# All 64 weighted sums as six full-fp32 products in two halves of the array's columns, and a plan without shifts

## The chip, the cores and the metric

The kernel runs on one core of a Trainium2 chip. The metric is the device time of one execution in microseconds, taken as the median over several runs. The core has a matrix engine (TensorE, PE in the profile; its weight loads are PEld), a vector engine (VectorE, DVE), a scalar engine (ScalarE, ACT), GpSimd (POOL) and a sync engine (SyncE, SP) that issues all DMAs here. They run side by side, each works through its own queue in order, and they wait for one another by semaphores. Matrix products are written to PSUM, eight banks of 512 fp32 columns on 128 partitions.

## The reference

```python
# attention: q, k, v are (8, 8, 576, 64), s is (8, 8, 576)
scores = scale * q @ k.T                      # causal, 576 x 576
cum    = cumsum(max(s, 0))
scores = where(causal, -1e9, scores + min(-(cum_i - cum_j), 0))
attn   = exp(scores - rowmax) / (rowsum + 1e-9)
x      = attn @ v                             # the weighted sum, 64 heads
# gated MLP on x as (8, 576, 512)
h      = gelu(x @ w_in)                       # 512 -> 1024
u, v   = halves of h;  v_n = layernorm(v) * g_ln
v_s    = w_sg @ v_n + b_sg                    # over the sequence
out    = x + (u * v_s) @ w_out
```

## The kernel before, in words

One head at a time is attended to, in batches of eight heads; the MLP ("ffn") of a batch runs while the heads of the next batches are worked on. For a head, `scores` forms q·k in pieces (PSUM tiles `pss`), adds the mask and takes the row extreme on VectorE, takes the exponential and its sum on ScalarE, and `norm` scales the rows by the reciprocal sums. `context` then makes the weighted sum. The probabilities (tiles `p`, and `e` for a third set that the first heads use) are transposed by TensorE in 13 blocks of 128x128 or smaller through two PSUM banks (`psp`), copied to SBUF (`pa`, `pb`, `pd`), and multiplied with the head's values (`vs`) into one PSUM bank (`psx`). The result is put into `xr`, half a tile per head. Queries are split in five row tiles and keys in five column tiles of 128 (the last of 64), and only the causal part is computed: the products have 512, 448, 320, 192, 64 and 64 columns.

The kernel has two ways to make that sum. The first 12 heads (`NP = 12`) use full fp32: the values are the stationary operand, 64 columns wide, and each product goes to one half of the array's columns (`side` 0 is PSUM partitions 0 to 63, `side` 1 is 64 to 127). The products come in two groups, the second of which ends with a product on 64 rows (`k=REM`). An fp32 product shows as two MATMUL records. The other 52 heads split every operand into a high and a low part in the reduced type fp32r: the values' high and low parts stand side by side in the 128 columns of the array (`split_v`, ScalarE and GpSimd), and the transposed probabilities' high and low parts (`pah`, `pal`, `pbh`, `pbl`, `pdh`, `pdl`) are streamed one after the other. That is ten products per head, spread over five steps, with the splitting on ScalarE and VectorE, and two more evacuations at the end. The MLP uses fp32r pairs as well (tiles `psm`), three products for each.

The order of the work is not the order of the code. All calls are collected in a `Plan` as operations with dependencies; the positions `POS` give the order in which they are collected. `Plan.order` simulates the five engines with the costs of `cost` and list-schedules them in a few rounds; `nc.group()` binds calls to one operation that nothing is put into. Before the last round each operation's priority is moved by an entry of the table `SHIFT` times 200 ns. The table unpacks to 7,972 entries between -45 and 45, and the 1,929 that are not zero all lie in the first 2,046. The order is then issued as it stands, so every engine's queue is fixed.

`norm` scales row tile 3 (448 columns) on ScalarE for the first 12 heads (`'n0': 'gggsg'`) and on GpSimd for the others (`'n': 'ggggg'`).

Of the kernel before, what the change touches and what calls it, by code (L numbers as in the profile page):

```python
# [64 lines left out]
SHIFT = (  # L65
    'c-rmM=gxu*wgq4mM4Amm6h#pWDzEo{Au5Vkuwg;Lf*?gWUruI{lbmF3V0`}Uto3_kfA)dhS0~s$EDC)_QP{?iA~VUw*M$%49_cZ|XV<;?@|v)&'
    '>R%GB9gu@xJ%e(`kP>!d$W7O$3N_DF^Y0W)G@Euz`D<%3JCd9Uw8pLbDi_q=?e>lfiO9bkl9IT}8_)0$`hp)JX3Z^6ZbqvO(v;?%{_G`;xu6GB'
    'oqSE+VoZHGE*!(IUo`jlmpKheeqIul+Cy%$x_gR+^5R8TP_x_pupXYwMi8>y)a9$8Z##=VP*7kL&ZHTqp?{_k%&JBFaY6FgmENDIe*}$v^5lR;'
    '%Su62Z01q8Q}4rTx4TdU9+QHdZz_?K2;?+qT>f(QXd!mr^=cLvf$h!tktHR&KAd$`o-{Hyc651S=ylG&%Z)|0nAZv9s1!MGb?iSHi1OAG7rSW2'
    '^UWl2m4)kWl6s_^XQTBAkt&VM2$-y4z1wZ-eAb=C^M*RZO602Du^Ym-XTI+*Hp(YoS12wA?a9yN)jnErup$;Nj*2w*Y!pMG{w{;lcbZM!jgM<&'  # L70
    'MPY`Q^60V(9oh^g916EeO@-8q(9d41g1xP4WE~u=<umpOwD2;YlxxFhGIOewYxkt9?N>PcW_Olc{0xsBnIsba5XM(1os?*@d&R%zakez8Sa#H?'
    '9llUN*F;&i`dSAX40E8N^a|0wy*YsHl&zkla><4@CV;^Q|MZ}&$W_vMuST04o@G;-Dt^TaQhMfVLX2$2eZ&^p#z-6@K<;)Xm~u0nd#Ptnsh8P%'
    '*JehSwnnwnz3EHP?#zcGvjL@DL^QclSwp9t%7i>VDdi4rl4Ys%xjlt|0H4QpM_neRlX*P}Wf1tg@YiAX$m)k)al8va5Y^n`G({g$eCy6G&hzK7'
    'd`$`ZCf!VtX1`}9`};pmqSniI%7xj&-JbTw->Eeftyaq^L1lATcE=Ywo1Sv9+AMc29J$*f8kT(4!_nSCx|I%98h#u#<+_dC8oibVG`sDD<CQ=z'
    'J)o9ZnLrZdN4CyO?boAKZA4!`k|vKzfKMB2?P>)c=ymX0^-K^>tCq`UU}xU=Lb_Lpy~8Apm6xoggPX#N=IMA&5dH>N4|s4gwqMP*pu||P*L1bn'
    'p!kBI%)ME0*8@x_s&8kQ1^CjgQo1FwxV^t1Q8*^4OmG|(xlv{Psj$UsbI%AdNIa0)mKbbDH0#&aD$^M|3lA?EC%N#q`Ka9|H_G59iun<2&|&Yr'
    'J+n;?uh6emE1mHx{r!9U@ZI-Pgm2?{9zF4QJ=W*OBGEh?x*|0&*`pXQTKU7PpKD-&bPGowcV{+Vgg>d4)SsWw)2LzTNQv)p5v_y$W$vsbAxTd('
    '{qcY+^OI=}K<v&wlvV$A4=Z^`f&uk_rg}YqrV34Y9FY){<Xfp~du3`#d9@<zJg4B=Jp7z*dSLmF!k=Z#ggQ3v*G>rU5X3-9m8CGPy}d8J5L23?'
    'i~Y?%-zuV7<N`KyCr$7|lR^x&XtZ-XG6-f9r<^WN+IZX{p?of5q>9weYwvbC^Jg=996_@3JTAQX<$x>;?O8l=Hv*cBMi{<Bg_4#!#N~NH!%$o='
    '43Dx$b4&D}y}z~)PU#5+>QJNmr?S(^XS7<McG%gNv-Q&TYaEcSS7l;CY|_5AG27t#<OIWQ_M{}ZQhT&4&S&92%QR=wZcx-{G*j6RS>`0hYg~F?'  # L80
    ')9CTKlU0_|y;1*VJ0)NlqKGzt4Iz?~H`>SIp4S%PD*v}~@LOU1$@PLAlU-p)5m?UDw*!t5E0=D9v@p2zw#dB*U+PupOwP>;s}~Y--|(N1d4H_j'
    '$jf_!nn3})wLJ%$WDLu`*Q_}2tMCxN**XZ8;xO?gaG^u0-@j7?+?N%=DJ8Oi2c(nE<As}NE0IVq96jxdL3FYMeX9e-9A#z^lzYB%c}R|Ycp1Am'
    '3|>4;iWlL^XYLW7V4<6|8X+*vQaQJlT{ak@Gv?MbDY&8adaF*9!ibi0zTeyruus6*JOGeg1XwzAEqcG)P&+-V_s_&$SSb3jD4+Iy05Gy<6DTmi'
    'y~1{>gxdxbH<1bn&Dypet{u$Pt+KiR5r#{?5AM^zw>dw4t8VD0z>K#4Zi1u<Tv7l5fItuU|FD$uzt<=L7GV6leRc-`Xa6gh{2llY(6~(epC|%9'
    'KR-V|KR-V|KR-V|KR-V|KR-V|KmWD<2cC(<Py'
)
# [245 lines left out]
def cost(o, eng, kind, outs, ins, kw):  # L332
    n = _cols(outs[0])
    if eng == "PE":
        w = _cols(kw["in_"] if kind == "transpose" else ins[0])
        if kind == "transpose":
            o.pes.append((85.0 * w / P, 58.0, 165.0))
        elif ins[0].dtype == F32R:
            o.pes.append((max(54.0, 0.836 * w), 0.4397 * n + 6.4, 165.0))
        else:  # L340
            x = 0.47 * n + 45 if w == D else 0.83 * n + 95
            o.pes.append((107.0, x, 0.0))
            o.pes.append((0.0, x, 90.0))
        return
# [57 lines left out]
def tile_attn_gmlp(  # L402
# [15 lines left out]
    class Ring:  # L418
# [11 lines left out]
        def __call__(self, shape, dtype, name, i=None, hold=False):  # L430
# [109 lines left out]
    def load_v(h):  # L540
        d = heads.setdefault(h, {})
        if h < NP:
            d["v"] = att.tile([P, 6, 2, D], F32, name="vf", tag="vs")[:, :, 0, :]
            nc.sync.dma_start(out=d["v"][:, 0:5], in_=vp[h, :, 0:5])
        else:
            d["vr"] = att.tile([P, 6, D], F32, name="vr", tag="vr", bufs=1)
            nc.sync.dma_start(out=d["vr"], in_=vp[h])
# [259 lines left out]
    def context(h):  # L807
        d = heads[h]
        pb = rbuf[pslot(h)]
        f32 = h < NP  # L810
# [10 lines left out]
        def new(name, w):  # L821
            return [att.tile([P, w], F32 if f32 else F32R, name=name + x, tag=name + x, bufs=1) for x in kinds]

        def evac(ts, c0, ps, w, e=nc.scalar):
            if f32:
                (e.copy if e is nc.scalar else e.tensor_copy)(out=ts[0][:, c0:c0 + w], in_=ps[:, 0:w])
            else:
                hi, lo = (t[:, c0:c0 + w] for t in ts)
                split(hi, lo, ps[:, 0:w], nc.scalar, nc.vector)

        def st(jt):
            return d["v"][:, jt, :] if f32 else d["vs"][:, jt, :, :].rearrange("p a d -> p (a d)")

# [13 lines left out]
        pb_ = new("pb", 768)  # L847
        evac(pb_, 0, t, 512, nc.vector)
        yield
        xx = ps_x.tile([P, 512], F32, name="xx", tag="xx")  # L850

        def mm(o0, o1, jt, m, side=0, k=P, **kw):
            o = xx[D * side:D * side + rows, o0:o1]
            nc.tensor.matmul(o, st(jt)[0:k], m, **{"start": False, "stop": False, **kw})

        if not f32:
            mm(0, 512, 0, pa[0], start=True)
# [14 lines left out]
        if f32:  # L872
            pd = [att.tile([P, 320], F32, name="pdh", tag="pdh", bufs=1)]
            nc.vector.tensor_copy(out=pd[0][0:64, 0:64], in_=t[0:64, 0:64])
            nc.vector.tensor_copy(out=pd[0][:, 64:320], in_=t[:, 64:320])
        else:
            hi, lo = pd = [att.tile([P, w], F32R, name="pd" + x, tag="pd" + x, bufs=1)
                           for x, w in (("h", 320), ("l", 192))]
            nc.scalar.copy(out=hi[0:64, 0:128], in_=t[0:64, 0:128])
            nc.scalar.copy(out=hi[:, 128:320], in_=t[:, 128:320])  # L880
            nc.vector.tensor_tensor(out=hi[64:128, 0:128], in0=t[0:64, 0:128], in1=hi[0:64, 0:128].bitcast(F32),
                                    op=ALU.subtract)
            nc.vector.tensor_tensor(out=lo, in0=t[:, 128:320], in1=hi[:, 128:320].bitcast(F32), op=ALU.subtract)
        yield
        if f32:
            with nc.group():
                mm(64, 512, 1, pb_[0][:, 320:768], side=1, start=True)
                mm(0, 512, 0, pa[0], start=True)
        else:
            with nc.group():  # L890
                for m in pb_:
                    mm(128, 448, 2, m[:, 0:320])
        yield
        if not f32:
            with nc.group():
                for m in pb_:
                    mm(64, 512, 1, m[:, 320:768])
# [5 lines left out]
        if f32:  # L903
            with nc.group():
                mm(128, 448, 2, pb_[0][:, 0:320], side=1)
                mm(192, 384, 3, pd[0][:, 128:320])
                mm(0, 64, 0, pd[0][:, 64:128], side=1, stop=True)
                mm(256, 320, 4, pd[0][0:REM, 0:64], k=REM, stop=True)
# [285 lines left out]
```

## Time and profile before

| | |
|---|---|
| median of 3 runs | 758.23 us (757.36 to 759.72) |
| span of the profiled execution, first to last instruction | 754.9 us |
| between the two | 3.3 us |
| TensorE busy | 743.1 us (98%) |
| VectorE, ScalarE, GpSimd busy | 594.8, 568.6, 573.7 us (79, 75, 76%) |
| granted TensorE clock, mean | 1.000 (2.4 GHz) |
| DMA queue's share of the 16 engines | 42.0% |

Busy time of TensorE counts a matmul from its start to its modelled end, and neighbours overlap; so the cost of a matmul is read from the distance between starts, not from its duration. All calls go through one helper, so that every instruction has the same line (L303), and groups are told apart by their tiles.

### The profile page before, as it was taken

What the parts mean: (1) busy time and instruction counts of PE and PEld (TensorE: products, weight loads), DVE (VectorE), ACT (ScalarE), POOL (GpSimd) and SP (SyncE); (2) the same over time, 40 slices, a digit from 0 to 9 for tenths busy, and PEclk for the clock granted to TensorE, in tenths of its full rate; (3) what the DMA queues carried; (4) which work ended last, traced back from release to release, by engine and by line L of the source; (5) the groups of instructions that cost most, each with busy time, mean ns of one, the idle gap of its engine ahead of it and who ended that gap; (6) DMA issues with size and microseconds to landing.
All of it is one profiled execution on the core that took longest, in us unless ns stands there. A gap on an engine that the chain in (4) does not pass through costs nothing.

```text
span 754.9 us, 16636 instructions
## 1 busy us (share of the span) xinstructions
PE 743.1 (98%) x5179; PEld 675.3 (89%) x5179; DVE 594.8 (79%) x1786; ACT 568.6 (75%) x1607; POOL 573.7 (76%) x954
## 2 busy tenths in 40 slices
PE   7999999999999999999999999999999999999998
PEld 4556779999999999999999999999999999999998
DVE  8999789668986788867797688967889678974752
ACT  5999999667985789857797588867888578862440
POOL 4789887967888687978789687896879868883641
PEclk9999999999999999999999999999999999999999
DMA  7776644345444344434443453443544444300101
GB/s 211 229 188 159 165 116 112 82 129 147 107 113 134 94 120 121 124 101 129 129 104 101 136 128 101 113 133 84 144 104 113 132 115 112 84 18 33 46 8 64
DMA packets 65388, 86.52 MB, mean 115 GB/s; under 512 B 24162, under 2 KB 40292, under 8 KB 65300
## 3 DMA queue, kind: packets, MB, share of 16 engines
q1 hardware_dynamic: 65300, 85.46, 42.0%
q8 instruction: 41, 0.67, 0.4%
q14 instruction: 47, 0.39, 0.2%
HBM read 39.50 MB, written 9.73 MB: 65 GB/s over the span
## 4 chain that ended last, share of the span: by engine, by line
PE 86%; ACT 5%; DVE 5%; DMA 2%; issue 1%; POOL 1%; SPq 0%; DVEq 0%; ACTq 0%; POOLq 0%
PE psm L303 52%; PE pss L303 13%; PE psx L303 12%; PE psp L303 9%; ACT p L303 2%; DVE psm L303 1%; DVE p L303 1%; DMA pair<-in_w_in 1%; DMA q<-k 0%; ACT pah L303 0%; DVE u L303 0%; ACT psm L303 0%; ACT e L303 0%; SPq L303 0%; DMA vs<-in_vp 0%
## 5 line engine op out<-in xcount | busy, mean ns | idle before, releaser
L303 POOL TENSOR_SCALAR p<-p,rs 128x320 f32<-128x320 f32 (+4 forms) x352 | 167.5, 483 | 31.0 <-DVE rs L303 14.2
L303 ACT ACTIVATE p<-p,mn 128x448 f32<-128x448 f32 (+3 forms) x300 | 167.8, 561 | 22.2 <-DVE mn L303 21.1
L303 PE MATMUL pss<-k,q 128*128 128x288 f32 (+9 forms) x768 | 151.4, 310 | 3.4 <-DVE mn L303 2.7
L303 PEld LDWEIGHTS pss<-k,q 128*128 128x128 f32 (+3 forms) x768 | 117.9, 180 | 23.8 <-DVE mn L303 6.9
L303 DVE CUSTOM_DVE_ANT_0 p<-pss,mask 128x448 f32<-128x448 f32 (+2 forms) x300 | 119.3, 419 | 19.0 <-PE pss L303 15.7
L303 PE MATMUL psm<-gt,wo 128*128 128x288 f32 x720 | 128.5, 301 | 0.0
L303 PE MATMUL psm<-xs,wi 128*128 128x288 f32 x720 | 121.2, 301 | 0.3 <-DVE u L303 0.2
L303 PE MATMUL psm<-ws,vn 128*128 128x288 f32 x708 | 120.6, 299 | 0.0
L303 PE MATMUL psm<-wi,xs 128*128 128x512 f32 (+1 forms) x380 | 108.3, 402 | 0.0
L303 POOL TENSOR_TENSOR k<-raw,k 128x576 fp32r<-128x576 f32 x56 | 80.3, 1433 | 36.1 <-ACT k L303 33.2
L303 PEld LDWEIGHTS psm<-gt,wo 128*128 128x128 f32 x720 | 105.8, 189 | 1.5
L303 PEld LDWEIGHTS psm<-xs,wi 128*128 128x128 f32 x720 | 102.5, 188 | 2.3 <-issue 0.8
L303 PEld LDWEIGHTS psm<-ws,vn 128*128 128x128 f32 x708 | 103.1, 188 | 1.3
L303 PEld LDWEIGHTS psp<-ident,r 128*128 128x128 f32 x780 | 84.5, 138 | 12.8 <-POOL p L303 1.7
L303 PE MATMUL psp<-ident,r 128*128 128x128 f32 x780 | 93.4, 240 | 1.6 <-ACT pbh L303 0.7
L303 POOL TENSOR_TENSOR gt<-u,gt 128x288 fp32r<-128x288 f32 (+1 forms) x66 | 53.1, 811 | 29.3 <-ACT gt L303 29.0
L303 PEld LDWEIGHTS psm<-wi,xs 128*128 128x128 f32 (+1 forms) x380 | 65.5, 184 | 10.3
L303 ACT CAST pbh<-psp 128x512 fp32r<-128x512 f32 (+1 forms) x104 | 49.4, 476 | 19.1 <-PE psp L303 18.3
L303 DVE TENSOR_TENSOR pbl<-psp,pbh 128x512 fp32r<-128x512 f32 (+1 forms) x104 | 56.9, 548 | 7.0 <-ACT pbh L303 6.4
L303 POOL TENSOR_TENSOR vs<-vr,vs 128x384 fp32r<-128x384 f32 x52 | 52.9, 1018 | 7.8 <-ACT vs L303 7.4
L303 ACT ACTIVATION_READ_ACCUMULATOR p<-p,mn 128x1 f32 (+1 forms) x300 | 57.5, 192 | 0.0
L303 PE MATMUL psx<-pbh,vs 128*128 128x320 f32 (+3 forms) x152 | 56.2, 402 | 0.7 <-ACT pbh L303 0.7
(151 smaller groups left out, 1571.0 us busy)
## 6 DMA issues: line engine op xcount, KB each, us to landing
q<-k SPq DMA_DIRECT2D x168, 144.0 KB
raw<-in_kq SPq DMA_DIRECT2D x56, 288.0 KB
vr<-in_vp SPq DMA_DIRECT2D x52, 192.0 KB
out_t<-u SPq DMA_DIRECT2D x64, 144.0 KB
k<-k SPq DMA_DIRECT2D x56, 144.0 KB
pair<-in_w_in SPq DMA_DIRECT2D x8, 512.0 KB
pair<-in_w_out SPq DMA_DIRECT2D x4, 512.0 KB
u<-xs SPq DMA_DIRECT2D x32, 64.0 KB
```

The source lines that it names most:

```text
L303: fn(*args, **kw)
```

## The change

Every head now makes its weighted sum in full fp32. `split_v`, the table of shifts and all fp32r parts of `context` go. The values are loaded once, as five tiles of 64 columns, into a ring of three; `pa` and `pb` get two buffers each; `pd` becomes a pair of fixed tiles whose lower left corner is zeroed once at the start. The four evacuations of the transposes become plain copies (two on ScalarE, three on VectorE, the last bank in two pieces). The six products form one group, alternating between the halves except for the fourth and fifth, and the product that used 64 rows uses 128. The end of a head is the one that the first 12 heads had: three copies on ScalarE, one addition on VectorE. `norm` runs on GpSimd for every head. In the planner's cost table the two records of such a product become 0.42 ns per column and 8 ns instead of 0.47 and 45, and its weight load 53 ns instead of 107. `SHIFT` is None.

```diff
-ENG = {'k': 'sg', 'vs': 'sg', ..., 'n': 'ggggg', 'n0': 'gggsg', 'ws1': 'g'}
-POS = dict(lk=-1.7, lkf=-1.55, lv=-1.35, lvf=-0.45, sk=-1.1, sv=-0.4, ..., cx=(1.0, 1.1, 1.2, 1.25, 1.35, 1.4, 1.45, 1.5), ...
+ENG = {'k': 'sg', ..., 'n': 'ggggg', 'ws1': 'g'}
+POS = dict(lk=-1.7, lkf=-1.55, lv=-0.9, sk=-1.1, ..., cx=(1.0, 1.1, 1.2, 1.25, 1.35, 1.4), ...
-SHIFT = ('c-rmM=gxu*...')
+SHIFT = None
-            x = 0.47 * n + 45 if w == D else 0.83 * n + 95
-            o.pes.append((107.0, x, 0.0))
+            x = 0.42 * n + 8 if w == D else 0.83 * n + 95
+            o.pes.append((53.0 if w == D else 107.0, x, 0.0))
-            ... "vr": (6 * D, 1), "vs": (12 * D, 2), ...
-            "pah": (512, 1), "pal": (512, 1), "pbh": (768, 1), "pbl": (768, 1), "pdh": (320, 1), "pdl": (192, 1),
+            ... "vf": (5 * D, 3), ...
+            "pa": (512, 2), "pb": (768, 2),
+    for i in range(2):
+        t = const.tile([P, 320], F32, name=f"pd_{i}")
+        nc.gpsimd.memset(t[D:P, 0:D], 0.0)
+        pds.append(t)
-            vs = d["vs"] = att.tile([P, 6, 2, D], F32R, name="vs", tag="vs")
-            split(vs[:, :, 0, :], vs[:, :, 1, :], d["vr"], *eng("vs"))
-            e = eng("n0" if h < NP else "n")[it]
+            e = eng("n")[it]
+        nc.scalar.copy(out=pa, in_=t)
...
+        nc.vector.tensor_copy(out=pk[:, 0:512], in_=t)
...
+        nc.scalar.copy(out=pk[:, 512:768], in_=t[:, 0:256])
...
+        nc.vector.tensor_copy(out=pd[0:64, 0:64], in_=t[0:64, 0:64])
+        nc.vector.tensor_copy(out=pd[:, 64:320], in_=t[:, 64:320])
...
+        with nc.group():
+            for o0, o1, jt, m, side, kw in ((64, 512, 1, pk[:, 320:768], 1, {"start": True}),
+                                            (0, 512, 0, pa, 0, {"start": True}),
+                                            (128, 448, 2, pk[:, 0:320], 1, {}),
+                                            (192, 384, 3, pd[:, 128:320], 0, {}),
+                                            (256, 320, 4, pd[:, 0:64], 0, {"stop": True}),
+                                            (0, 64, 0, pd[:, 64:128], 1, {"stop": True})):
+                nc.tensor.matmul(xx[D * side:D * side + D, o0:o1], v[:, jt, :], m, ...)
```

## Rows read from the trace of the kernel before

**Rows 1.** The page, busy time and share of the span by engine.
```profile
PE 743.1 (98%) x5179; PEld 675.3 (89%) x5179; DVE 594.8 (79%) x1786; ACT 568.6 (75%) x1607; POOL 573.7 (76%) x954
```
**Rows 2.** Busy time by stretch of the span, instructions, granted clock, DMA.
```profile
core 0: us, PE busy (x) PEld busy (x) DVE busy (x) ACT busy (x) POOL busy (x), PEclk, DMA share, GB/s
...
20.00:40.00 20.00, 18.49 (x102) 10.88 (x101) 19.77 (x65) 19.08 (x57) 14.96 (x23) 1.00 0.77 223
40.00:60.00 20.00, 18.99 (x105) 11.23 (x104) 18.46 (x63) 19.87 (x61) 17.84 (x27) 1.00 0.68 172
60.00:80.00 20.00, 18.91 (x122) 13.92 (x123) 17.41 (x52) 19.06 (x56) 18.59 (x27) 1.00 0.68 178
...
429.40:518.30 88.90, 88.90 (x642) 84.19 (x641) 71.50 (x220) 69.73 (x201) 71.78 (x119) 1.00 0.44 117
```
**Rows 3.** The chain that ended last: start, length, what.
```profile
58.14 1.68 ACT p L303 x5
...
63.98 1.80 PE psx L303 x11
...
340.50 3.88 PE psm L303 x20
...
429.41 3.88 PE psm L303 x20
```
**Rows 4.** TensorE's timeline at 389 to 392 us: start, length, tiles, count.
```profile
389.46 1.22 PE L303 MATMUL psm<-xs,wi 128*128 128x288 f32 x8
390.52 0.43 PE L303 MATMUL pss<-k,q 128*128 128x288 f32 x2
...
391.32 0.81 PE L303 MATMUL psp<-ident,r 128*128 128x128 f32 x8
391.97 0.44 PE L303 MATMUL pss<-k,q 128*128 128x448 f32 x1
```
**Rows 5.** TensorE's timeline, one fp32r head's products at 452 us.
```profile
452.07 0.39 PE L303 MATMUL psx<-pah,vs 128*128 128x512 f32 x1
...
453.38 0.51 PE L303 MATMUL psm<-gt,wo 128*128 128x288 f32 x2
453.73 0.19 PE L303 MATMUL psp<-pdh,vs 128*128 128x64 f32 x1
...
453.93 0.68 PE L303 MATMUL pss<-k,q 128*128 128x448 f32 x4
```
**Rows 6.** TensorE's timeline, an fp32 head whose two groups adjoin.
```profile
86.00 0.59 PE L303 MATMUL psx<-pbh,vs 128*64 128x448 f32 x1
86.00 0.64 PE L303 MATMUL psx<-pah,vs 128*64 128x512 f32 x1
86.42 0.54 PE L303 MATMUL psx<-pbh,vs 128*64 128x448 f32 x1
...
86.80 0.43 PE L303 MATMUL psx<-pbh,vs 128*64 128x320 f32 x1
...
87.07 0.43 PE L303 MATMUL psx<-pbh,vs 128*64 128x320 f32 x1
...
87.80 0.88 PE L303 MATMUL psp<-ident,r 128*128 128x128 f32 x8
88.52 0.38 PE L303 MATMUL pss<-k,q 128*128 128x320 f32 x1
```
**Rows 7.** TensorE's timeline, an fp32 head whose groups stand apart.
```profile
107.56 1.10 PE L303 MATMUL psm<-xs,wi 128*128 128x288 f32 x7
108.58 0.59 PE L303 MATMUL psx<-pbh,vs 128*64 128x448 f32 x1
...
109.59 2.52 PE L303 MATMUL psm<-xs,wi 128*128 128x288 f32 x17
112.05 0.48 PE L303 MATMUL psx<-pbh,vs 128*64 128x320 f32 x1
...
113.10 0.80 PE L303 MATMUL pss<-k,q 128*128 128x288 f32 x4
```
**Rows 8.** ScalarE's groups from 20 to 62 us.
```profile
L303 ACT ACTIVATE p<-p,rs 128x448 f32<-128x448 f32 x5 | 3.3, 659 | 0.0
```
**Rows 9.** GpSimd's groups from 62 to 115 us.
```profile
L303 POOL TENSOR_SCALAR p<-p,rs 128x448 f32<-128x448 f32 x1 | 0.6, 641 | 0.0
```

More of the change, by code (lines that the diff above doesn't have):

```diff
@@ L55 @@
 NI = 2
-NP = 12
 U2 = 7
-ENG = {'k': 'sg', 'vs': 'sg', 'xs': 'gg', 'ln': 'sg', 'gt': 'sg', 'w': 'gg', 'ws': 'sg', 'n': 'ggggg', 'n0': 'gggsg', 'ws1': 'g'}
-POS = dict(lk=-1.7, lkf=-1.55, lv=-1.35, lvf=-0.45, sk=-1.1, sv=-0.4, sc=(0, 0.15, 0.3, 0.4), cx=(1.0, 1.1, 1.2, 1.25, 1.35, 1.4, 1.45, 1.5), wv=(0.1, 6.0), wu=(5.0, 9.0),
+ENG = {'k': 'sg', 'xs': 'gg', 'ln': 'sg', 'gt': 'sg', 'w': 'gg', 'ws': 'sg', 'n': 'ggggg', 'ws1': 'g'}
+POS = dict(lk=-1.7, lkf=-1.55, lv=-0.9, sk=-1.1, sc=(0, 0.15, 0.3, 0.4), cx=(1.0, 1.1, 1.2, 1.25, 1.35, 1.4), wv=(0.1, 6.0), wu=(5.0, 9.0),
            ws=(8.5, 11.0), wo=(8.6, 9.8), f0=9.7, x0=2.4)
@@ L63 @@
 ROUNDS = 5
[L65 to L86, printed above, removed]
+SHIFT = None
 N3 = 12
@@ L461, in tile_attn_gmlp @@
     RING = {"p0": (PW[0], 2, False), "p1": (PW[1], 2, False), "p2": (PW[2], 2, False), "p3": (PW[3], 2, False), "p4": (PW[4], 2, False),
-            "k1": (S, 2), "q1": (S, 2), "k2": (S, 2), "raw": (S, 1), "vr": (6 * D, 1), "vs": (12 * D, 2), "mn": (5, 2), "rs": (5, 2),
-            "pah": (512, 1), "pal": (512, 1), "pbh": (768, 1), "pbl": (768, 1), "pdh": (320, 1), "pdl": (192, 1),
+            "k1": (S, 2), "q1": (S, 2), "k2": (S, 2), "raw": (S, 1), "vf": (5 * D, 3), "mn": (5, 2), "rs": (5, 2),
+            "pa": (512, 2), "pb": (768, 2),
             "xr": (S, XR), "xs": (2 * S, 4), "vt": (512, 2), "vn": (1024, 4), "vnr1": (512, 1), "u2": (CH, U2), "gt": (2 * CH, 5),
@@ L541, in load_v @@
         d = heads.setdefault(h, {})
[L542 to L547, printed above, removed]
+        d["v"] = att.tile([P, 5, D], F32, name="vf", tag="vf")
+        nc.sync.dma_start(out=d["v"], in_=vp[h])
     dram = ctx.enter_context(tc.tile_pool(name="dram", bufs=1, space=bass.MemoryType.DRAM))
@@ L595, in tile_attn_gmlp @@
     sums = []
+    pds = []
+    for i in range(2):
+        t = const.tile([P, 320], F32, name=f"pd_{i}")
+        nc.gpsimd.memset(t[D:P, 0:D], 0.0)
+        pds.append(t)
     for i in range(3):
@@ L705, in split_k @@
         nc.sync.dma_start(out=k2[64:66, :].bitcast(F32), in_=cum[:, h, :])
-    def split_v(h):
-        d = heads[h]
-        if h >= NP:
-            vs = d["vs"] = att.tile([P, 6, 2, D], F32R, name="vs", tag="vs")
-            split(vs[:, :, 0, :], vs[:, :, 1, :], d["vr"], *eng("vs"))
     def qk_part(h, it, pst, c0, j0, j1, start=True):
@@ L809, in context @@
         pb = rbuf[pslot(h)]
-        f32 = h < NP
-        kinds = "h" if f32 else "hl"
-        rows = D if f32 else P
+        v = d["v"]
         c, half = h % H // 2, h % 2
@@ L819, in tr @@
             nc.tensor.transpose(out=ps[0:n, o:o + P].bitcast(F32R), in_=pb[it][:, jb:jb + n], identity=ident)
[L821 to L832, printed above, removed]
         t = bank()
@@ L837, in context @@
                 tr(t, o, it, 0)
-        pa = new("pa", 512)
-        evac(pa, 0, t, 512)
+        pa = att.tile([P, 512], F32, name="pa", tag="pa")
+        nc.scalar.copy(out=pa, in_=t)
         yield
@@ L846, in context @@
             tr(t, 128, 4, 256)
[L847 to L857, printed above, removed]
+        pk = att.tile([P, 768], F32, name="pb", tag="pb")
+        nc.vector.tensor_copy(out=pk[:, 0:512], in_=t)
         yield
@@ L862, in context @@
             tr(t, 0, 4, 128)
-        evac(pb_, 512, t, 256)
-        if not f32:
-            mm(0, 512, 0, pa[1])
+        nc.scalar.copy(out=pk[:, 512:768], in_=t[:, 0:256])
         yield
@@ L871, in context @@
             tr(t, 192, 4, 384)
[L872 to L883, printed above, removed]
-        yield
[L885 to L897, printed above, removed]
+        pd = pds[h % 2]
+        nc.vector.tensor_copy(out=pd[0:64, 0:64], in_=t[0:64, 0:64])
+        nc.vector.tensor_copy(out=pd[:, 64:320], in_=t[:, 64:320])
+        yield
+        xx = ps_x.tile([P, 512], F32, name="xx", tag="xx")
+        with nc.group():
[5 more added lines that the diff above has]
+                                            (0, 64, 0, pd[:, 64:128], 1, {"stop": True})):
+                nc.tensor.matmul(xx[D * side:D * side + D, o0:o1], v[:, jt, :], m,
+                                 **{"start": False, "stop": False, **kw})
         yield
@@ L902, in context @@
         hs = slice(D * half, D * half + D)
[L903 to L908, printed above, removed]
-            with nc.group():
-                nc.scalar.copy(out=xt[hs, 0:64], in_=xx[64:128, 0:64])
-                nc.scalar.copy(out=xt[hs, 64:128], in_=xx[0:64, 0:64])
-                nc.scalar.copy(out=xt[hs, 128:S], in_=xx[64:128, 64:512])
-            nc.vector.tensor_tensor(out=xt[hs, 128:S], in0=xx[0:64, 64:512], in1=xt[hs, 128:S], op=ALU.add)
-        else:
-            x0 = bank()
-            mm(192, 384, 3, pd[0][:, 128:320])
-            mm(256, 320, 4, pd[0][:, 0:64])
-            with nc.group():
-                nc.tensor.matmul(x0[:, 0:64], st(5), pd[0][:, 64:128], start=True, stop=True)
-                mm(192, 384, 3, pd[1], stop=True)
-            for ps, o, sl in ((x0, slice(0, 64), slice(0, 64)), (xx, slice(0, 512), slice(64, S))):
-                nc.scalar.copy(out=xt[hs, sl], in_=ps[64:128, o])
-                nc.vector.tensor_tensor(out=xt[hs, sl], in0=ps[0:64, o], in1=xt[hs, sl], op=ALU.add)
+        with nc.group():
+            nc.scalar.copy(out=xt[hs, 0:64], in_=xx[64:128, 0:64])
+            nc.scalar.copy(out=xt[hs, 64:128], in_=xx[0:64, 0:64])
+            nc.scalar.copy(out=xt[hs, 128:S], in_=xx[64:128, 64:512])
+        nc.vector.tensor_tensor(out=xt[hs, 128:S], in0=xx[0:64, 64:512], in1=xt[hs, 128:S], op=ALU.add)
         del heads[h]
@@ L1121, in tile_attn_gmlp @@
             place(h + POS["lkf" if h < NQ else "lk"], load_k, h)
-            place(h + POS["lvf" if h < NP else "lv"], load_v, h)
+            place(h + POS["lv"], load_v, h)
         place(h + POS["sk"], split_k, h)
-        place(h + POS["sv"], split_v, h)
         for g, key in ((sc, "sc"), (cx, "cx")):
@@ L1158, in _layout @@
     kq = np.concatenate([k.transpose(0, 2, 1), q.transpose(0, 2, 1)[:, :, tok]], axis=1)
-    v6 = np.concatenate([v, v[:, NT * P:], v[:, 0:REM], v[:, 0:REM]], axis=1)
+    v5 = np.concatenate([v, v[:, NT * P:]], axis=1)
     def bits(a):
@@ L1164, in _layout @@
         "kq": kq,
-        "vp": v6.reshape(BH, 6, P, D).transpose(0, 2, 1, 3),
+        "vp": v5.reshape(BH, 5, P, D).transpose(0, 2, 1, 3),
         "s_t": i["s"].reshape(BH, S),
```

## The prediction

> **What bounds the kernel now.** I read the page's busy shares first: TensorE is busy 98% of the span, the other three engines under 80% [rows 1]. An average hides stages, so the busy time by stretch comes next. Two regimes show. From about 62 us on TensorE is the bound: in a stretch the length of a batch it is busy 88.90 of 88.90 us, the others about 70 [rows 2]. From 20 to 60 us it is not: VectorE is busy 19.77 of 20 in the first half, ScalarE 19.87 of 20 in the second, and TensorE leaves 1.5 and 1.0 us open [rows 2]. The chain says the same: it runs through ScalarE up to some 62 us and through TensorE from there, and it repeats with the batch: the same piece stands at 340.50 and at 429.41 us, 88.9 us apart [rows 3]. The granted clock is 1.00 in all these stretches, the 2.4 GHz level [rows 2]. So what the change does to a head past the start is worth what it does to TensorE's own time, and all that is taken from ScalarE, VectorE and GpSimd there is worth nothing by itself.
>
> TensorE's prices I take from distances between starts. Eight MLP products of 288 columns take 1.06 us from the first to the next instruction, so 0.1325 each; eight transposes take 0.65 us [rows 4].
>
> **The change, part by part.**
>
> *The ten fp32r products of heads 12 to 63 go.* One head shows them almost together [rows 5]. The first eight take 453.38 - 452.07 = 1.31 us. The two MLP products behind them take 0.35 us where two cost 0.265, since a 64-column product is over before the next weights are loaded: 0.085. The last two take 0.20. Sum 1.60 us of TensorE per head. Nothing else of it is on the path.
>
> *One run of six fp32 products comes.* The fp32 heads of the start show its parts. The two halves of the array do run side by side: a 448-column and a 512-column product start at the same 86.00 [rows 6]. On half 1 the two records of 448 columns are 0.42 and 0.38 us apart, the records of 320 columns 0.27 [rows 6], which is 0.84 ns per column and record, so 0.05 for 64 columns. In the new run half 1 has 448, 320 and 64 columns, 832, and half 0 has 512, 192 and 64, 768; the longer sets the length: 0.42 + 0.38 + 2 x 0.27 + 2 x 0.05 = 1.45 us. Leaving costs a pause: the pair alone lasts 109.59 - 108.58 = 1.01 us [rows 7], where 512 columns at 0.84 ns twice, with the 0.05 that the first record has on top (0.42 against 0.38), make 0.91; so 0.10. That gives 1.55 us from the first start to the next instruction. (The old run of all ten records took 87.80 - 86.00 = 1.80 [rows 6]; the 0.25 too many are the 64-row product, which stands alone at the end.) Its neighbours pay too. Seven MLP products ahead of a run take 1.02 us instead of 0.93: 0.09 to enter. Seventeen between two runs take 2.46 instead of 2.25: 0.21, which is 0.09 to enter the second and some 0.10 behind the first [rows 7]. In full 1.55 + 0.09 + 0.10 = 1.74 us between MLP products. That is the upper bound. Eight transposes behind a run take 0.72 instead of 0.65 [rows 4, 6], and if a run also stood behind transposes, whose next instruction waits for weights anyhow, the entry could be free: 1.55 + 0.07 = 1.62, the lower bound. Of the twenty runs and part runs of the start, 5 come behind transposes and 11 before; I take 1.70.
>
> So a head past the start costs TensorE 0.10 us more (0.02 to 0.14): 52 x 0.10 = **+5.2 us** (+1.0 to +7.3).
>
> *Heads 0 to 11 get the one run.* From the sixth head on they lie where TensorE is the bound. Three of these seven have adjoining groups, 1.80 against 1.55: 0.25 each. Four have them apart: 1.01 and 1.05 [rows 7] with twice 0.19 around them, 2.44 against 1.74: 0.70 each. 3 x 0.25 + 4 x 0.70 = **-3.55 us**.
>
> *The start, heads 0 to 4.* The scaling of row tile 3 leaves ScalarE, 0.659 us each, five of them between 20 and 62 us: 3.3 us of the engine that ends last [rows 8]. It lands on GpSimd at 0.641 [rows 9], which has 17.84 of 20 us in use in the second half of that stretch and 18.59 in the one after [rows 2]; some three heads per 20 us bring it to 19.8 and 20.5, full. VectorE has less than 2 us open in each. So one engine's relief meets another's limit, and I take **0**, between -3.3 (all of ScalarE's time) and +1.5 (GpSimd over its limit in three such stretches by 0.5).
>
> *The plan has no shifts.* They reach only the first quarter of the operations, which is the start and the two batches after it. No row prices them. Below: nothing, if the order found without them is as good. Above: what TensorE has open between 20 and 60 us, 2.5 us, once more [rows 2]. I take **+1.0**.
>
> *Splits, low parts, extra evacuations, a second buffer for `pa` and `pb`.* Their cover past the start is TensorE, with 17 us per batch to spare on each engine [rows 2]: 0. If TensorE were not the bound, they would be a gain. The value load moves behind the five DMAs of the key split, one issue as before, with 160 KB instead of 192; it is needed more than a head later, 11 us: 0. Two small memsets at the start: 0.
>
> *The new wait.* The run's first product waits for all copies of the head, on ScalarE and VectorE, and everything TensorE has behind it waits along, both the MLP and the next scores. The plan has MLP products to put ahead of it: 0; its price is a rival below.
>
> Sum: 5.2 - 3.55 + 0 + 1.0 = **+2.65 us**, from 754.9 to 757.5 us of span. The runs lie 3.3 us above the span at their median of 758.2, so **760.9 us**, 0.35% more.
>
> **The rivals.**
>
> *The ends of a run are hidden where TensorE is dense.* Then a run costs 1.55, less than the 1.60 that goes. Steady state 52 x -0.05 = -2.6; the seven early heads 3 x 0.44 + 4 x 0.89 = -4.9; with +1.0 that is -6.5, **751.7 us, faster**. It decides below some 1.62 us per run. For it: half the start's rows come from stretches with waits. Against: the pauses are the same where TensorE was dense [rows 7]. The Trainium skill's "TensorE: Matmul & The Clock Gate", section "Measured speedup vs the span model", goes further, since products in different tiles of the array should take one product's time and 4 ns for each further tile, with no price for entering; by that a run is 1.45 us and the whole some 746 us. The trace disagrees, with 0.09 and 0.10 at either end, and rather bears out "Mode switching requires drain" of "TensorEngine Tiling (Array Packing)", section "Key Properties".
>
> *The start pays.* All 3.3 us of ScalarE's relief come through: 757.6 us, no change that can be told.
>
> *The run waits.* If VectorE's last copy is 0.1 us late for each of the 52 runs, that is +5.2: 766 us. Against it: VectorE is idle a fifth of the time and gets less to do [rows 2].
>
> *The halves do not overlap in the new run.* Then its 1,600 columns take 2 x 1.34 us, 52 x 1.2 us more: about 823 us. The equal starts speak against it [rows 6].
>
> **How the numbers follow.** A change within 0.3% (2.3 us) can't be told from none here. The forecast (758.5 to 763) gets 0.50, of which 0.32 is slower by more than 0.3%; the hidden ends 0.16; the paying start 0.17, of which 0.04 is faster; the waiting run, or a start that GpSimd holds up, 0.15; no overlap 0.02. So faster 0.20, same 0.31, slower 0.49. The range has to reach both signs: 753 to 766, which leaves out the better half of the hidden ends and the worse part of the waits. The forecast's own range is 758.5 to 763.
>
> **What would show it.** In the profile after: a run from first start to next instruction of 1.55 us, with MLP neighbours 0.09 and 0.10 longer; a batch 0.8 us longer than 88.9; TensorE still busy throughout; the other engines some 15 us lower per batch; GpSimd near 20 of 20 between 40 and 80 us. I am wrong if the batch is shorter than 88.9, if TensorE waits at the runs, or if the start before 115 us moves by more than 5 us.

## The result and the profile after

The changed kernel takes 763.31 us (median of 8 runs, 760.99 to 764.90); beside it the kernel before took 758.99 (8 runs, 757.36 to 760.78). The ratio is 1.0054, with a 95% interval of 1.0038 to 1.0071: slower, by more than the 0.3% that can be told from nothing. The forecast of 760.9 had the sign and lies 2.4 us low; as a change, +2.65 was forecast and +4.3 measured.

The page's busy line of after, to be held against [rows 1]:

```profile
PE 744.7 (98%) x5283; PEld 657.3 (86%) x5283; DVE 532.2 (70%) x1630; ACT 510.1 (67%) x1439; POOL 529.2 (69%) x916
```

VectorE, ScalarE and GpSimd lost 63, 59 and 45 us of work, and the span grew from 754.9 to 761.7 us all the same. TensorE's busy time grew by 1.6 us and its idle time, span less busy, from 11.8 to 17.0. So of 6.8 us of span only a quarter is more work on TensorE. (The spans differ by more than the medians, 4.3 us. The profiled execution of after took 763.5 us, 1.8 around its span. The runs of before whose spans are on record lie 2.0 us above them, so the profiled one was at some 756.9, an estimate, below its median of 759. The 3.3 us that I put around the span held this luck.)

Where the idle time lies, the busy time by stretch says. After, with the stretches of [rows 2] and one batch of the steady part:

```profile
core 0: us, PE busy (x) PEld busy (x) DVE busy (x) ACT busy (x) POOL busy (x), PEclk, DMA share, GB/s
...
0.00:120.00 120.00, 106.17 (x622) 78.01 (x623) 103.47 (x327) 98.94 (x285) 100.43 (x174) 0.97 0.62 173
...
20.00:40.00 20.00, 17.53 (x104) 11.60 (x102) 19.93 (x64) 17.35 (x54) 16.19 (x26) 1.00 0.73 213
40.00:60.00 20.00, 17.62 (x106) 11.36 (x105) 19.81 (x68) 18.62 (x58) 16.99 (x27) 1.00 0.62 178
60.00:80.00 20.00, 19.65 (x134) 15.60 (x134) 16.53 (x51) 17.58 (x55) 19.16 (x29) 1.00 0.69 177
80.00:100.00 20.00, 16.49 (x96) 12.69 (x94) 13.08 (x44) 15.22 (x44) 19.10 (x34) 0.91 0.50 125
...
434.25:523.89 89.64, 89.64 (x658) 80.69 (x657) 62.38 (x196) 62.02 (x178) 63.88 (x111) 1.00 0.43 113
```

The same view of the kernel before, two stretches that [rows 2] do not have:

```profile
0.00:120.00 120.00, 111.79 (x645) 77.00 (x646) 106.83 (x331) 107.00 (x303) 93.33 (x159) 1.00 0.65 175
...
80.00:100.00 20.00, 19.48 (x121) 14.64 (x121) 16.47 (x54) 18.87 (x51) 16.73 (x31) 1.00 0.57 137
```

In the first 120 us TensorE leaves 13.8 us open (idle) after the change and 8.2 before: that is all of the new idle time, and 3.0 of it lie between 80 and 100 us, where the granted clock is 0.91 instead of 1.00. In the steady part TensorE is busy 89.64 of 89.64 us.

The chain of after (start, length, what) repeats there with the batch, as it did in [rows 3]:

```profile
344.61 4.72 PE psm L281 x25
...
432.70 1.55 PE psx L281 x11
434.25 4.72 PE psm L281 x25
...
523.89 4.72 PE psm L281 x25
```

The batch is 89.64 us long, before 88.91: 0.73 more, 0.09 for each of its eight heads. The order has a part in this: the kernels below with all heads in one run repeat after 89.21 to 89.88 us, those with fp32r in heads 12 to 63 all after 88.9. One run of six products, in TensorE's timeline of after:

```profile
432.28 0.43 PE L281 MATMUL pss<-k,q 128*128 128x288 f32 x2
432.63 0.59 PE L281 MATMUL psx<-pb,vf 128*64 128x448 f32 x1
432.64 0.64 PE L281 MATMUL psx<-pa,vf 128*64 128x512 f32 x1
...
433.71 0.54 PE L281 MATMUL psx<-pd,vf 128*64 128x192 f32 x5
434.18 1.72 PE L281 MATMUL psm<-ws,vn 128*128 128x288 f32 x11
435.74 0.30 PE L281 MATMUL psm<-wr,vnr 128*128 128x288 f32 x1
```

From 432.63 to 434.18 are 1.55 us. The two products ahead take 0.35 where two of 288 columns cost 0.265 [rows 4]: 0.09 to enter. The eleven behind take 1.56 instead of 1.46: 0.10. These are the forecast's numbers.

### The profile page after: what moved, and what is told of

Its sections match the earlier page's. It is cut to its first block, busy times and chain, and to the rows that moved or that the text cites. A ratio compares the mean times of both kernels' runs of the same rounds, so it can differ in the third digit from the quotient of the medians.

```text
span 761.7 us, 16375 instructions
## 1 busy us (share of the span) xinstructions
PE 744.7 (98%) x5283; PEld 657.3 (86%) x5283; DVE 532.2 (70%) x1630; ACT 510.1 (67%) x1439; POOL 529.2 (69%) x916
## 4 chain that ended last, share of the span: by engine, by line
PE 88%; DVE 6%; POOL 3%; DMA 2%; issue 1%; SPq 0%; ACT 0%; POOLq 0%; DVEq 0%
PE psm L281 53%; PE pss L281 14%; PE psx L281 11%; PE psp L281 9%; DVE psm L281 1%; DVE p L281 1%; DMA pair<-in_w_in 1%; POOL e L281 1%; DVE e L281 1%; DMA q<-k 1%; POOL k L281 1%; SPq L281 0%; DVE gt L281 0%; POOL xs L281 0%; DVE pb L281 0%
## 5 line engine op out<-in xcount | busy, mean ns | idle before, releaser
L281 ACT ACTIVATE p<-p,mn 128x448 f32<-128x448 f32 (+1 forms) x300 | 166.9, 558 | 46.3 <-DVE mn L281 43.2
L281 POOL TENSOR_SCALAR p<-p,rs 128x448 f32<-128x448 f32 x360 | 172.2, 485 | 37.0 <-DVE rs L281 18.4
L281 DVE CUSTOM_DVE_ANT_0 p<-pss,mask 128x448 f32<-128x448 f32 (+1 forms) x300 | 119.2, 421 | 39.7 <-PE pss L281 35.9
L281 PE MATMUL psm<-gt,wo 128*128 128x288 f32 x720 | 121.4, 301 | 0.0
L281 PE MATMUL psx<-pb,vf 128*64 128x448 f32 (+1 forms) x256 | 96.3, 498 | 0.7 <-ACT pb L281 0.7
L281 PE MATMUL psp<-ident,r 128*128 128x128 f32 x780 | 89.9, 242 | 2.3 <-ACT pa L281 1.8
L281 ACT COPY xr<-psx 64x64 f32<-64x64 f32 (+1 forms) x192 | 60.2, 314 | 29.1 <-PE psx L281 26.8
L281 PEld LDWEIGHTS psm<-wi,xs 128*128 128x128 f32 (+1 forms) x380 | 67.3, 186 | 13.1 <-POOL xs L281 0.9
L281 PE MATMUL psx<-pa,vf 128*64 128x512 f32 x128 | 68.5, 616 | 0.0
L281 DVE SCALAR_TENSOR_TENSOR u<-u,psm 128x288 f32<-128x288 f32 x120 | 52.4, 442 | 15.7 <-ACT u L281 13.1
L281 PEld LDWEIGHTS psx<-pb,vf 128*64 128x64 f32 x256 | 29.8, 136 | 36.3 <-issue 31.4
```

The costliest lines, as they stand in the source:

```text
L281: fn(*args, **kw)
```

## The experiments

Twelve more kernels ran. Ratios are to the kernel before, run beside them, with 95% intervals.

### From before to after in four rungs

The first three kernels, put between before and after, take the change apart.

**The table of shifts alone.** The kernel before with one edit:

```diff
-SHIFT = ('c-rmM=gxu*...')
+SHIFT = None
```

> The kernel before with SHIFT = None and nothing else. Theory 'order': the changed kernel lost its start (about 5 us more than forecast, worst between heads 7 and 9) because the plan has no shifts; then this kernel is 2 to 4 us slower than before, 761 to 763 us, with a period of 88.9 us per batch kept. Rival 'GpSimd': the start was lost because the scaling of row tile 3 went to GpSimd; then this kernel is within 1 us of before, since that scaling is still on ScalarE here.

Measured: 760.93 us, ratio 1.0050 (1.0031 to 1.0068), 3.8 us. The steady part is untouched (the chain's piece stands at 344.17 and 433.08 us, 88.91 apart), so all of it is lost in the start. I had +1.0, with 2.5 as upper bound.

**Heads 0 to 11 in one run, and no shifts.** Heads 12 to 63 stay fp32r.

```diff
-SHIFT = ('c-rmM=gxu*...')
+SHIFT = None
-            x = 0.47 * n + 45 if w == D else 0.83 * n + 95
-            o.pes.append((107.0, x, 0.0))
+            x = 0.42 * n + 8 if w == D else 0.83 * n + 95
+            o.pes.append((53.0 if w == D else 107.0, x, 0.0))
...
+                mm(128, 448, 2, pb_[0][:, 0:320], side=1)
+                mm(192, 384, 3, pd[0][:, 128:320])
+                mm(256, 320, 4, pd[0][:, 0:64], stop=True)
+                mm(0, 64, 0, pd[0][:, 64:128], side=1, stop=True)
...
-            with nc.group():
-                mm(128, 448, 2, pb_[0][:, 0:320], side=1)
...
```

> The kernel before with SHIFT = None, and heads 0 to 11 make their sum in the one run of six (same cost numbers as in the change); heads 12 to 63 keep the ten fp32r products. By the forecast's second term, 3.55 us faster than the kernel that only lacks the shifts, with 1.55 us from a run's first start to the next instruction and 88.9 us per batch. Rival: the start is not held by TensorE up to 115 us, and it is equal to that kernel within 1 us.

Measured: 760.78 us, ratio 1.0043 (1.0026 to 1.0059). Against the rung before it that is 0.1 to 0.5 us, not 3.55. Where the gain went, the first line of the page and the first 120 us show. The kernel without shifts:

```profile
PE 745.7 (98%) x5179; PEld 676.4 (89%) x5179; DVE 594.4 (78%) x1786; ACT 568.5 (75%) x1607; POOL 572.5 (75%) x954
...
0.00:120.00 120.00, 111.07 (x629) 75.56 (x630) 103.94 (x324) 105.60 (x296) 91.55 (x156) 1.00 0.61 169
```

and the one with the first 12 heads in one run:

```profile
PE 741.7 (98%) x5179; PEld 678.7 (90%) x5179; DVE 593.7 (78%) x1786; ACT 567.7 (75%) x1607; POOL 572.6 (76%) x955
...
0.00:120.00 120.00, 106.93 (x620) 76.35 (x620) 103.67 (x322) 104.01 (x294) 91.56 (x159) 0.99 0.61 168
```

TensorE's work fell by 4.0 us, about as forecast, and its open time in the first 120 us rose from 8.9 to 13.1. The saving arrived and was not used. Where it is lost, VectorE's additions into `xr` show, which end a head (start and length). Heads 7 and 9 without shifts:

```profile
81.41 0.62 DVE L282 TENSOR_TENSOR xr<-psx,xr 64x448 f32<-64x448 f32 x1
...
100.30 0.62 DVE L282 TENSOR_TENSOR xr<-psx,xr 64x448 f32<-64x448 f32 x1 [0.54 <-ACT xr L282]
```

and with the first 12 heads in one run:

```profile
77.49 0.62 DVE L282 TENSOR_TENSOR xr<-psx,xr 64x448 f32<-64x448 f32 x1 [1.19 <-ACT xr L282]
...
105.18 0.62 DVE L282 TENSOR_TENSOR xr<-psx,xr 64x448 f32<-64x448 f32 x1
```

Head 7 ends 3.9 us earlier, head 9 4.9 us later, and head 12 at 129.3 us in both. So TensorE does not set the pace at heads 8 and 9, whatever was gained before them. (The planner's price changed with the run, and the order with it.)

**Tile 3 back on ScalarE.** After, with `norm` as it was for the first 12 heads. Beside the rung above, heads 12 to 63 are now in one run as well, with all else of the change.

```diff
-ENG = {..., 'n': 'ggggg', 'ws1': 'g'}
+ENG = {..., 'n': 'ggggg', 'n0': 'gggsg', 'ws1': 'g'}
-            e = eng("n")[it]
+            e = eng("n0" if h < 12 else "n")[it]
```

> The changed kernel with the scaling of row tile 3 on ScalarE again for heads 0 to 11. Theory 'GpSimd': GpSimd falls from 19.1 to some 17 of 20 us between 60 and 100 us, TensorE's idle time and the low clock at 92 us go, and it is 2 to 4 us faster than the changed kernel, 759 to 761 us. Theory 'order': within 1 us of the changed kernel, 762 to 764 us. Both: 89.64 us per batch as in the changed kernel.

Measured: 766.64 us, ratio 1.0100 (1.0084 to 1.0115), 7.6 us. So leaving `norm` alone is not better but 3.3 us worse than the change, and the theory that GpSimd holds the start falls: it has 10 us less to do in the first 120 (90.39 against 100.43), and TensorE is as open as in after, 13.2 us against 13.8. From 80 to 100 us the clock is lower still:

```profile
80.00:100.00 20.00, 17.44 (x84) 13.21 (x83) 12.71 (x44) 16.19 (x45) 16.70 (x34) 0.74 0.49 127
```

TensorE is busier here than in after and gets 84 products done instead of 96: busy time at a lower clock is not progress.

The four rungs, by ratio of 758.5 us: no shifts +3.8; early heads in one run -0.5; all other heads in one run +4.3; tile 3 to GpSimd -3.5; together +4.1. Each ratio is good to some 1.3 us, a step between two of them to some 1.8.

A part of these steps goes with the clock, whose mean is on record for each run. At 1.000 the kernel without shifts took 760.04 to 760.58 us (three runs), and before, over all comparisons, 756.46 to 759.09 (eleven runs, median 757.94): 2.4 us apart and not 3.8. The kernel with tile 3 on ScalarE had three of its five runs at 0.991, 766.64 to 766.80; at 0.998 and 0.997 it took 763.56 and 764.53, where after took 762.22 and 763.12 at 0.997: 1.4 us apart and not 3.5.

### The ends of a run

**Two groups instead of one** (after, with the six products as 2 and 4, and a position in `cx` for each). If the ends were hidden, this would cost nothing.

```diff
-        with nc.group():
-            for o0, o1, jt, m, side, kw in (... six products ...):
+        for part in (six[:2], six[2:]):
+            with nc.group():
+                for o0, o1, jt, m, side, kw in part:
...
+            yield
```

> The changed kernel with each head's six products in two groups (the first pair, then the other four), so that the plan may put other work between them. Theory 'the ends of a run cost TensorE': each head whose groups stand apart pays entry 0.09, pause 0.10, a slower follower 0.10 and a first weight load 0.05 once more, 0.34 us; if all 64 do, 22 us slower than the changed kernel (785 us), if half do, 11 us. Rival 'the ends are hidden where TensorE is dense': within 2 us of the changed kernel.

Measured: 777.40 us, ratio 1.0261 (1.0244 to 1.0278). The chain of this kernel:

```profile
345.91 2.97 PE psm L281 x21
...
436.52 3.00 PE psm L281 x21
```

90.61 us per batch, 0.97 more than after, which makes some 6 of the 14 us; the rest is lost in the start. In this batch the groups of two of the eight heads come apart, at 444.29 and 471.50 us. Their parts take 1.01 and 0.80 us where a run takes 1.55, 0.26 more, and a second pair of ends at 0.19 makes 0.45 per head: 0.9 of the 0.97. The ends are not hidden.

**The six products in bf16** (16-bit floats), still in halves of the columns.

```diff
+            "vr": (5 * D, 3)
...
+        d["vr"] = att.tile([P, 5, D], BF16, name="vr", tag="vr")
+        nc.scalar.copy(out=d["vr"], in_=d["v"])
-        pa = att.tile([P, 512], F32, name="pa", tag="pa")
+        pa = att.tile([P, 512], BF16, name="pa", tag="pa")
...
```

> The changed kernel with the values and the transposed probabilities rounded to bf16 (an extra copy per head on ScalarE makes the values), so that each of the six products is one pass on the same halves of the columns; the output has bf16's precision in the weighted sums. It measures what the ends of a run belong to. If the halves cost the pause: a run is some 0.35 + 0.05 + 0.10 = 0.50 us from first start to next instruction, MLP neighbours still take 0.22 us ahead and 0.23 behind instead of 0.13. If full fp32 costs it: some 0.40 us and neighbours at 0.13 to 0.14. In both cases about 70 us less TensorE time, so a kernel near 690 to 700 us if nothing else becomes the bound.

A single run: 732.28 us, beside 758.81 of before. TensorE's timeline:

```profile
240.28 1.35 PE L281 MATMUL psm<-gt,wo 128*128 128x288 f32 x9
241.56 0.38 PE L281 MATMUL psx<-pb,vr 128*64 128x448 bf16 x1
241.56 0.40 PE L281 MATMUL psx<-pa,vr 128*64 128x512 bf16 x1
241.77 0.30 PE L281 MATMUL psx<-pb,vr 128*64 128x320 bf16 x1
...
242.03 1.20 PE L281 MATMUL psm<-gt,wo 128*128 128x288 f32 x7
```

The nine products ahead take 1.28 us instead of 1.19: the same 0.09 to enter. The run takes 0.47 us; at 0.21 for 448 columns its longer half's 832 make 0.39, so 0.08 of pause are left. (The runs from 430 to 526 us take 0.45 to 0.48.) The ends belong to the halves of the columns, not to fp32. They are a price per run, 0.3 us with the slower follower, whatever the run holds.

This kernel says the most about the start. Each head needs 1.08 us less of TensorE, and the batch shrinks by 5.6 of the 8.6 us freed (its chain repeats after 84.06 us, and TensorE is busy 82.29 of them, so something else now holds a part of the batch). But in the first 120 us TensorE is busy 100.92 us, at a mean clock of 0.89, and the heads there end no earlier. A start that cannot use 1 us per head cannot use 0.25 to 0.70 either.

**The run behind transposes.** After, with each run held back until the next head's first four transposes, where the forecast's lower bound had the entry free.

```diff
-cx=(1.0, 1.1, 1.2, 1.25, 1.35, 1.4)
+cx=(1.0, 1.1, 1.2, 1.25, 1.35, 2.05)
...
+            if h:
+                late.pop(h - 1)()
-            place(8 * b + max(2 * c + 2.6, ...), xsplit, b, c)
+            place(8 * b + max(2 * c + 3.2, ...), xsplit, b, c)
```

> The changed kernel with each head's run bound behind the first four transposes of the next head, in one group. By the lower bound of the forecast a run behind transposes enters free; so 0.07 to 0.09 us per head less: a batch 0.6 to 0.7 us shorter, 88.9 to 89.1 us, and 4 to 5 us off the whole, 758 to 759.5 us, if the start does not get worse by the later end of each head. Rival 'entry costs the same after transposes': 89.6 us per batch, within 1 us of the changed kernel or slower.

Measured: 763.55 us, ratio 1.0064 (1.0049 to 1.0078), level with after. The batch is 89.87 us (432.37 to 522.24), and TensorE waits in it, 39.53 of 40 us busy between 480 and 520. Together with the second key buffer below the batch comes down:

> The two edits together (second raw buffer, runs behind transposes). If both theories hold, 754 to 757 us, faster than both kernels; if only the key chain holds, 759 to 761; if only the entry, 758 to 760.

Measured: 764.69 us, ratio 1.0073 (1.0058 to 1.0088). The batch is 89.21 us (435.90 to 525.11), 0.43 less than after. But the entry is not what went. All eight runs of this batch stand behind four transposes, which take 0.39 us up to the run; four transposes ahead of MLP products take 0.29:

```profile
458.86 0.46 PE L281 MATMUL psp<-ident,r 128*128 128x128 f32 x4
459.15 1.69 PE L281 MATMUL psm<-gt,wo 128*128 128x288 f32 x11
...
481.03 0.46 PE L281 MATMUL psp<-ident,r 128*128 128x128 f32 x4
481.42 0.59 PE L281 MATMUL psx<-pb,vf 128*64 128x448 f32 x1
```

That is 0.10 to enter, as behind MLP products. Where the 0.43 come from is not shown; the order alone moves the batch by some tenths (89.77 us with tile 3 on ScalarE, 347.71 to 437.49 in its chain). Over some six and a half batches 0.43 would be 2.8 us; the start lost more than that.

### What holds the start

In after, the first wait that grows is at the ninth and tenth head. TensorE's timeline (idle before, and what ended it, in brackets):

```profile
86.06 0.59 PE L281 MATMUL psx<-pb,vf 128*64 128x448 f32 x1 [0.69 <-ACT pb L281]
...
90.33 0.37 PE L281 MATMUL psp<-ident,r 128*128 128x128 f32 x2 [1.57 <-ACT pa L281]
90.55 0.44 PE L281 MATMUL pss<-k,q 128*128 128x448 f32 x1
91.37 1.23 PE L281 MATMUL pss<-k,q 66*128 66x448 f32 x7 [0.38 <-DMA k<-cum]
...
92.74 2.89 PE L281 MATMUL psm<-wi,xs 128*128 128x512 f32 x6
95.42 0.53 PE L281 MATMUL pss<-k,q 128*128 128x288 f32 x2
```

ScalarE, SyncE's queue and GpSimd, which feed it:

```profile
83.55 1.42 POOL L281 TENSOR_TENSOR k<-raw,k 128x576 fp32r<-128x576 f32 x1
...
85.00 0.36 SPq L281 DMA_DIRECT2D raw<-in_kq  x1
...
89.03 0.67 ACT L281 CAST k<-raw 128x576 fp32r<-128x576 f32 x1 [0.77 <-PE psp L281]
...
89.72 0.56 ACT L281 COPY pa<-psp 128x512 f32<-128x512 f32 x1
```

There is one buffer `raw` for loaded keys. The next load is issued at 85.00, when GpSimd has read the last ones; ScalarE casts them at 89.03, and the copy of `pa`, for which TensorE waits, stands behind that cast in ScalarE's queue. (The profile names a transpose as the cast's releaser; the cast reads nothing of it, so I put this wait down to the load. In the chain of the second rung such a load takes 4.27 us from 70.89, and the cast behind it starts at 75.23; from 85.00 to 89.03 are 4.03.) Then the clock: six products of 512 columns take 2.68 us from 92.74 to 95.42, 0.45 each, where before four took 1.00 at the same place:

```profile
90.99 1.16 PE L303 MATMUL psm<-wi,xs 128*128 128x512 f32 x4
91.99 0.43 PE L303 MATMUL pss<-k,q 128*128 128x288 f32 x2
```

**A second buffer for the keys.** After, with two buffers `raw` and the load 0.9 of a head earlier.

```diff
-POS = dict(lk=-1.7, ...
+POS = dict(lk=-2.6, ...
-            ... "raw": (S, 1), ...
+            ... "raw": (S, 2), ...
```

> The changed kernel with a second buffer for the raw keys and queries of heads 8 to 63, which are loaded 0.9 of a head earlier. Theory 'key chain': at heads 8 and 9 ScalarE's cast of the raw keys waits in its queue for a load that could not be issued before GpSimd was done with the only buffer, and the copies of the transposes stand behind it, so TensorE idles and its clock falls to half at 92 us; with two buffers these waits go and it is 2 to 4 us faster than the changed kernel, 759 to 761 us, granted clock 1.00 from 80 to 100 us. Rival 'GpSimd is simply full': within 1 us of the changed kernel. Both: 89.6 us per batch.

Measured: 761.68 us, ratio 1.0035 (1.0022 to 1.0047). The stall at the ninth head goes:

```profile
80.00:100.00 20.00, 18.85 (x126) 15.11 (x125) 16.02 (x59) 17.33 (x53) 19.44 (x36) 1.00 0.56 140
```

126 products instead of 96 in this stretch, at full clock, and 1.6 us in the end. The clock falls elsewhere, to 0.91 between 60 and 80 us, behind a wait of 2.0 us for GpSimd (`xs`), and some of what was won is waited for later. The wait was real, and it was not the last one.

**Price and shifts.** After with a dearer run in the planner's table (`0.42 * n + 32`, which makes it 1.73 us, close to what it costs):

> The changed kernel with the planner's price of a run put right: 32 ns instead of 8 beside the 0.42 ns per column, 1.73 us for the six products as measured, where the change has 1.44. Theory 'price': the plan put the start together for runs that are 0.3 us shorter than they are, and with the right price it is 1 to 3 us faster, 760.5 to 762.5 us. Rival 'shifts alone': within 1 us of the changed kernel.

Measured: 768.84 us, ratio 1.0126 (1.0109 to 1.0143). A truer price made the kernel 5.5 us slower; the theory that the planner errs by the cheap run falls. Not all of it is start: in this kernel and the two that follow the batch is 89.88 us (here 335.66 to 425.54 in the chain), 0.24 more than after, and TensorE once waits 0.5 to 0.7 us for a DMA near 490 us. Over six and a half batches that is some 2 us, an estimate. The same kernel with a new table `SHIFT`, the best by the planner's own estimate among random ones:

> The kernel with the right price, and a new table of shifts for its first 2,046 operations, found by trying random tables in the kernel's own planner. Theory 'shifts': the table that the change dropped was worth 3 to 4 us on the old plan and a new one is worth the same here: 759 to 760.5 us, that is before plus the steady cost (4.6 us) less what the one run saves in the start. Rival 'the start of the changed kernel is worse for another reason': no better than 762 us.

Measured: 762.62 us, ratio 1.0051 (1.0035 to 1.0067): 6.2 us off, by order alone. With the second buffer for the keys as well, and a table of its own:

> As the last, with the second raw buffer and the earlier load of the keys, and a table of its own. If key chain and shifts add up, 757 to 759 us, level with before; if the shifts already work round the chain, the same as the last within 1 us. 89.6 us per batch.

Measured: 760.77 us (12 runs), ratio 1.0026 (1.0014 to 1.0039), the best of the kernels with all heads in fp32, and still not level with before; the 2 us of its steady part are about what is missing. Last, the kernel before with its first 12 heads in one run, the dearer price and a new table:

> The kernel before with heads 0 to 11 in the one run and heads 12 to 63 in fp32r, the right price, and a new table of shifts. If TensorE holds the start once the order is good, the forecast's second term comes through and it is 2 to 3.5 us faster than before, 755 to 757 us. If the start is held by the chain to the first split keys at heads 8 and 9 whatever TensorE saves, it is level with before within 1.5 us. 88.9 us per batch.

Measured: 758.34 us (13 runs), ratio 0.9991 (0.9980 to 1.0003). The 3.55 us do not come with a table of shifts either. At full clock some 1 us of them is there: its two runs at 1.000 took 756.70 and 757.14, below before's 757.94. But seven of its 13 runs stand at 0.995, and one of the 23 of before beside them.

## Why the prediction was right in sign and off in its parts

**What bounds the kernel: right past the start, wrong before 115 us.** The steady part behaves as TensorE's bound. But I read the start's end at 62 us, from the chain and from 88.90 of 88.90 in one batch, while [rows 2] show TensorE at 18.91 of 20 between 60 and 80. The chain of before, read on past 62 us, leaves TensorE once more:

```profile
78.95 2.36 DMA vs<-in_vp
...
81.32 1.44 POOL k L303
...
83.78 3.70 DMA q<-k
...
87.50 1.41 DMA k<-cum
```

For 10 us it runs through the load of the values, GpSimd's part of the key split and the DMAs of the split keys, where after has its waits. So between 62 and 120 us TensorE is nearly full and not always the bound. My own sign of being wrong, a start that moves by more than 5 us, came true in part: by the ends of the additions into `xr` heads 9 and 11 (counted from 0) are 5.7 and 6.5 us late, head 12 only 1.2.

**The steady heads: right.** Predicted +5.2 us; 0.09 per head times 52 is 4.7, and the rung that holds it measured +4.3. Run, entry and follower are 1.55, 0.09 and 0.10, as worked out. The lower bound is out: behind transposes the entry costs as much. The other three engines fell by 8 to 9 us per batch, not by 15; that figure had no working behind it. It cost the forecast nothing, for the time they gave back is idle time.

The Trainium skill's "Key Properties" in "TensorEngine Tiling (Array Packing)" says that a change of tiling mode drains TensorE. The trace agrees, with 0.09 and 0.10 at the ends of each run, in fp32 and in bf16; that a drain is all that passes there, no run shows. By the span model in the Trainium skill's "TensorE: Matmul & The Clock Gate" ("Measured speedup vs the span model") a run would have come to 1.45 us, an estimate from the rows of one half; the runs of after's batch from 434 us on all take 1.55.

**Heads 5 to 11, -3.55: the step that failed.** The saving is there as TensorE's work (4.0 us less between the first two rungs) and not as time: -0.5 in that rung, and no difference in the last experiment, whose interval holds 1 (some 1 us at full clock). I took TensorE for the bound of these heads. What releases TensorE at heads 8 and 9 is the chain from the load of the keys through ScalarE's queue.

**Tile 3 to GpSimd, 0: mis-sized.** The rung measured -3.5, at the lower bound, -3.3; at like clock it is some 1.4. GpSimd did fill up as I said (19.16 of 20 from 60 to 80 us) but lightening it left TensorE as open, 13.2 us against 13.8; only single waits end with it (0.8 us for `xs` between 80 and 120 us). That the 3.5 are ScalarE's relief and not a luckier order is not shown: a change of price alone moved the kernel by 5.5.

**No shifts, +1.0: mis-sized.** It measured +3.8, outside my bounds of 0 and 2.5 (2.4 at full clock). I bounded it by the open time of TensorE between 20 and 60 us; the start that an order can worsen is longer.

**The new wait, 0: right** in the steady part, where TensorE has no idle time; in the start a run does wait once, 0.69 us at 86.06.

So the sum of the start's three terms was -2.55 and came as -0.2, out of three errors of 3, -3.5 and 2.8 us; with the steady term's -0.9 they leave +1.45. That so little was left is luck. The sign came from the steady term alone. Of the rivals, "the start pays" had its price about right and lost to the shifts and the early heads, which it took as the forecast had them; "ends hidden" is out by the 0.09 and 0.10 beside the run and by the two groups, "the run waits" by TensorE's 89.64 of 89.64 us, "no overlap" by the runs of 1.55 us.

Of the start's losses, how much is the order of the work and how much the clock that falls with its pauses is not settled; no run held one of the two fixed. The runs at the highest clock allow an estimate: after took 760.99 and 761.16 us at 1.000 and 0.999, 3.1 above before's 757.94 at 1.000, where the medians are 4.3 apart. So some 1.2 of the 4.3 go with the clock.

## What to carry to other kernels

A term of work saved on the busiest engine counts only in stretches where that engine is also the one that others wait for; read that for each stretch, by what ends its waits, not by a busy share of 95%. An order tuned by hand or by table is worth several microseconds of its own, so a change that has to drop it should be priced with the table dropped from the old kernel first. Products on half of the array's columns paid about 0.3 us per run at its ends here, so they belong together.

## What the runs showed of the hardware

A pause of TensorE is paid twice in this kernel. In after's profile the granted clock of the stretch behind the pauses at 88.8 us is half, the 1.2 GHz level, though no pause was longer than 1.57 us. The rows of the stretch behind the pauses, and of the one with the longest:

```profile
92.30:95.50 3.20, 3.20 (x12) 2.62 (x12) 2.09 (x10) 2.35 (x9) 3.10 (x13) 0.50 0.73 198
88.80:90.30 1.50, 0.00 (x0) 0.00 (x0) 1.50 (x5) 1.25 (x3) 1.06 (x2) 1.00 0.44 113
```

The six products there cost 0.45 us each instead of 0.25, so 1.2 us more. The runs of one kernel also follow it: after took 760.99 us at a mean granted clock of 1.000, 763.12 at 0.997, 764.23 at 0.995 and 764.90 at 0.993; the other four lie between. Most of the 0.5% between runs of one program goes with it.
